# Two PSUM banks for the row products, one for the transposes, and an order that knows banks, in a fused attention and two-layer kernel

## The chip, the cores and the metric

The program runs on one core of a Trainium2 chip. The metric is the device time of one execution in microseconds (us): median of three runs for the kernel before, 859.1 us (858.09 to 859.74).

The engines are named as the profile names them: PE (matrix multiply), PEld (its weight loads), DVE (vector), ACT (scalar), POOL (GpSimd, which issues nearly all loads here) and SP (which issues DMA transposes and the last stores).

## What is computed

Block-causal attention over 4 batches of 8 heads (576 positions, head size 64), then two feed-forward layers over the 2304 tokens:

```python
scores = scale * np.matmul(q, k.transpose(0, 1, 3, 2))
scores = np.where(block_i >= block_j, scores, -1000000000.0)   # blocks of 64
attn = np.exp(scores - np.max(scores, axis=-1, keepdims=True))
attn = attn / (np.sum(attn, axis=-1, keepdims=True) + 1e-09)
x = np.matmul(attn, v)                     # 2304 tokens x 512
h = ((x @ w1) * (x @ w2)) @ w3             # 1024
x = h @ w_out                              # 512
r = np.maximum(x @ w_in, 0.0)              # 2048
out = (r * r) @ w2_out                     # 512
```

Weights come as float64 words and are turned into high and low parts on the chip, so a product is three matmuls (high x high, high x low, low x high).

## The kernel before

**Order.** Nothing is issued where the code stands. Every step is recorded in a list (`od.op`, class `Order`) with its engine, a cost, the keys it reads and writes, and a priority. At the end `Order.emit` plays the list through a small model of the engines: it takes the ready step with the lowest priority key on the engine that is free first, and issues it. So each engine has one fixed order of instructions, set by the costs in the model, and on the chip each engine runs its own list strictly in that order. A tile (`Buf`) belongs to a tag with a number of buffers; a new tile of a tag waits for the last user of the tile that many places before it. In the model of before two engines may work in one PSUM bank as long as the keys differ. On the chip they wait for each other there.

**Setup and batch 0.** The first attention pairs 0 to 3 (batch 0, two heads each) are `whole`: scores `s` on PE (line 825), maxima on DVE, exponentials on ACT (line 884), scaling by the reciprocal on DVE (line 910), transposes of the weights on PE (`tp`, line 968) into a PSUM bank, a copy of that bank to `pt` on ACT (line 974), then the product with v (`pv_bank`, line 1071). The transposes of one head and one group of query tiles come in two parts, each with its own `tp` tile. The tag `tp` has two banks, the tag `po` one.

Between them stand the rows `setup_rows(i)`, i = 0 to 7: row i of w3 times w_out, on PE at line 1108, output `po`, then copied out as a high part by ACT (line 1209) and a low part by DVE (line 1214) into `w3o`. Rows 0 to 2 use float32 operands, which show as two trace instructions for each matmul. Row 0 takes the whole `po` bank. Rows 1 to 5 take the same single `po` bank in two halves of 256 columns. Rows 6 and 7 and everything after take banks in turn from the two `tp` and the one `po` (`bank3`).

The 64-bit words of w_out (`wo`), w3 (`w3t`) and w1, w2 (`w`) are loaded by POOL, scaled on ACT (lines 325, 329, 478, 483) and joined on DVE. Where PE has nothing to do in the first 25 us the model issues `warm_up` matmuls (line 591), which compute nothing.

**Batches 0 to 3.** From about 122 us the products `ab` with w1 and w2 start, and attention of the next batch runs beside them. Each of the eight w1/w2 tiles needs a column sum on PE (line 357, input `wsum`) in the midst of the PE list.

**Second layer.** From about 490 us the 2304 rows of y are worked off in blocks c = 0 (256 columns) and c = 1 to 4 (512 columns), each in eight steps j. Blocks 2 to 4 use seven products instead of eight (`h_winograd`, line 1866; `out_strassen`, line 2034). `y_load(c)` makes from the loaded y the parts b11, b21, t1, t2, t3, t4, b22, each as a high part (ACT, line 275) and a low part (DVE, line 277); each part has one buffer, which every block uses again.

## Time and profile before

| what | value |
|---|---|
| median of three runs | 859.1 us |
| the profiled execution | 859.63 us |
| its span, first to last instruction | 857.9 us |
| PE busy | 834.0 us (97%) |
| DVE busy | 704.3 us (82%) |
| ACT busy | 605.3 us (71%) |
| POOL busy | 111.4 us (13%) |

PE is the engine that is nearly always busy. A row of the timeline reads: start, length, engine, line, operation, output and inputs with shapes, how many instructions are merged, and in brackets the idle time ahead of the first of them with what ended it. Matmul rows are modelled at their ends and overlap a little.

### The profile page before, as it was taken

To read this page: it belongs to the slowest core of one execution; us is meant where nothing else is said; L and a number is where in the kernel's file an instruction comes from. 1 tells how busy PE (TensorE), PEld (TensorE's weight loads), DVE (VectorE), ACT (ScalarE), POOL (GpSimd) and SP (SyncE) were. 2 spreads that over 40 slices of the span, in tenths; PEclk is the share of its full clock that TensorE was granted. 3 is DMA by queue.
4 is the path that set the end of the run, shared out by engine and by line. 5 is a ranking of instruction groups with operands and counts; after the bars stand their busy time and mean duration, and the time that the engine had idled before them with its cause. 6 is when DMAs were issued, how large, how long until landed. Compare 5 with 4: busy or idle time off the path is not lost. (4 is left out here: it accounts for less than half of the span.)

```text
span 857.9 us, 19317 instructions
## 1 busy us (share of the span) xinstructions
PE 834.0 (97%) x7504; PEld 676.9 (79%) x7504; DVE 704.3 (82%) x1643; ACT 605.3 (71%) x1393; POOL 111.4 (13%) x206
## 2 busy tenths in 40 slices
PE   8999999999999999999999999999999999999997
PEld 6567776778878888789979878666678888888886
DVE  5988989997787787864788899999979798797775
ACT  5988888976677676764999985756755654664562
POOL 5111211111211112001322101010020001001000
PEclk9999999999999999999999999999999999999999
DMA  8942465699998999772665512020030002001001
GB/s 312 339 150 93 135 176 161 143 182 191 215 178 159 196 154 202 134 148 77 210 193 191 176 50 74 26 100 2 1 109 16 1 2 74 2 1 51 1 2 50
DMA packets 104830, 100.23 MB, mean 117 GB/s; under 512 B 83041, under 2 KB 86881, under 8 KB 103329
## 3 DMA queue, kind: packets, MB, share of 16 engines
q0 software_dynamic: 18144, 71.18, 26.5%
q1 hardware_dynamic: 86592, 27.80, 19.1%
q8 instruction: 59, 0.97, 0.5%
q14 instruction: 35, 0.28, 0.1%
HBM read 62.78 MB, written 9.44 MB: 84 GB/s over the span
## 5 line engine op out<-in xcount | busy, mean ns | idle before, releaser
L1108 PEld LDWEIGHTS <-w 128*128 128x128 f16 x1536 | 146.8, 98 | 43.7 <-issue 5.9
L884 ACT ACTIVATE pf<-s,nm 128x192 f32<-128x192 f32 (+4 forms) x160 | 82.4, 524 | 44.0 <-DVE nm L867 39.5
L1108 PE MATMUL ab<-x0h,w 128*128 128x320 f16 x512 | 108.9, 299 | 0.5 <-DVE w L287 0.3
L1108 PE MATMUL y<-g,w3o 128*128 128x320 f32 (+1 forms) x768 | 108.3, 298 | 0.0
L1108 PEld LDWEIGHTS y<-g,w3o 128*128 128x128 f32 x768 | 103.1, 188 | 2.1 <-issue 1.2
L1108 PE MATMUL ab<-x1h,w 128*128 128x256 f16 x512 | 88.7, 273 | 0.0
L2034 PEld LDWEIGHTS <-gs 128*128 128x128 f16 x816 | 78.9, 98 | 11.4 <-DVE gs L277 2.2
L1866 PEld LDWEIGHTS <-wb 128*128 128x128 f16 x768 | 75.1, 98 | 15.2 <-issue 3.8
L1108 PE MATMUL ab<-x0l,w 128*128 128x320 f16 x256 | 76.5, 299 | 0.7 <-DVE x0l L1033 0.7
L1929 ACT ACTIVATE c<-c,beta 128x512 f32<-128x512 f32 x48 | 34.2, 713 | 58.4 <-DVE c L1898 58.4
L932 DVE SCALAR_TENSOR_TENSOR p<-pf,r,p 128x192 f16<-128x192 f32 (+2 forms) x120 | 63.0, 546 | 12.5 <-ACT p L925 11.2
L1108 PE MATMUL ab<-x1l,w 128*128 128x256 f16 x256 | 69.8, 272 | 0.0
L2161 PE MATMUL o<-wb,g 128*128 128x512 f16 x288 | 66.7, 379 | 0.6 <-DVE c L2171 0.6
L925 ACT ACTIVATE p<-pf,r 128x192 f16<-128x192 f32 (+2 forms) x120 | 62.0, 556 | 6.6 <-DMA pt<-p 3.7
L2034 PE MATMUL p<-ts,gs 128*128 128x256 f16 x480 | 61.8, 273 | 0.1
L1866 PEld LDWEIGHTS <-st 128*128 128x128 f16 x576 | 56.1, 98 | 6.7
L825 PE MATMUL s<-kraw,qraw 64*128 64x288 f32 (+4 forms) x384 | 56.5, 411 | 0.4 <-ACT pf L884 0.2
L2161 PEld LDWEIGHTS <-g 128*128 128x128 f16 x288 | 27.9, 98 | 30.3 <-issue 0.9
L825 PEld LDWEIGHTS s<-kraw,qraw 64*128 64x128 f32 x384 | 34.2, 186 | 17.1 <-issue 8.3
L2034 PE MATMUL p<-wb,gs 128*128 128x256 f16 x336 | 44.7, 273 | 0.2 <-DVE gs L277 0.2
L859 DVE TENSOR_REDUCE nm<-s 128x2 f32<-128x384 f32 (+1 forms) x64 | 42.3, 683 | 1.0
L338 DVE CUSTOM_DVE_ANT_0 cx<-raw,cx 128x1024 uint16<-128x1024 uint16 (+1 forms) x53 | 39.0, 737 | 4.5 <-ACT raw L329 2.3
(265 smaller groups left out, 1977.4 us busy)
## 6 DMA issues: line engine op xcount, KB each, us to landing
raw<-in_wb POOLq DMA_DIRECT2D x32, 512.0 KB, 5.5
raw<-in_w3t POOLq DMA_DIRECT2D x8, 1024.0 KB, 10.0
raw<-in_w POOLq DMA_DIRECT2D x16, 512.0 KB, 4.8
yraw<-ydram POOLq DMA_DIRECT2D x12, 512.0 KB, 4.5
vraw<-in_vp POOLq DMA_DIRECT2D x16, 320.0 KB, 5.3
qraw<-in_qT POOLq DMA_DIRECT2D x16, 288.0 KB, 4.7
kraw<-in_kT POOLq DMA_DIRECT2D x32, 144.0 KB, 5.9
vmix<-v SPq DMA_DIRECT2D x24, 160.0 KB, 5.0
```

The source lines that it names most:

```text
L338: dve.tensor_tensor(out=x(), in0=x(), in1=words()[1], op=ALU.add)
L825: pe.matmul(o[:, h] if t == 4 else o, q()[rows, q_start(t) : q_start(t) + 128], keys_()[rows, c], start=True, stop=True,)
L859: lambda k=k, t=t, nm=nm, banks=banks: dve.tensor_reduce(out=nm()[:, k], in_=banks[0]()[:, :, S_COL[t] : S_COL[t] + n_keys(t)], op=ALU.max ...
L884: act.activation(o, view(a, t), AF.Exp, bias=nm()[:, k, a : a + 1], scale=SCALE, accum_out=ssum()[:, k, a : a + 1],)
L925: lambda o=o, nk=nk, a=a, k=k, w=weights, p16=p16, r=r: act.activation(p16()[:, o : o + nk], w(a, k), AF.Copy, scale=r()[:, k, a : a + 1]),
L932: lambda o=o, nk=nk, a=a, k=k, w=weights, p16=p16, r=r: dve.scalar_tensor_tensor(out=p16()[:, o + nk : o + 2 * nk], in0=w(a, k), scalar=r( ...
L1108: pe.matmul(acc(), l, r, start=k == 0, stop=k == len(mms) - 1)
L1866: pe.matmul(acc()[:, TH * half : TH * half + TH], lhs(a, kc), y[yn]()[:, kc], start=n == 0, stop=n == len(mms) - 1,)
L1929: lambda src=src, k=k: act.activation(src(), src(), AF.Relu, scale=beta()[:, j, k : k + 1]),
L2034: pe.matmul(acc()[:, TH * u : TH * u + TH], t()[:, o : o + P], r(b), start=first and n == 0 and u == tiles[0], stop=last and n == 2 and u ...
L2161: pe.matmul(o(), g[gx]()[:, cols], wt(f)[:, a, 512:1024], start=(begin and n == 0), stop=(last and n == 2),)
```

## The change

1. `PSUM_POOLS`, `Op.banks`, `at` and `held`: the model keeps, for each PSUM bank, until when each engine works in it, and lets no other engine start there before.
2. `c_first`: a faster cost for loads (0.55 to issue, 0.00245 per KB, 2.3 to land, before 0.6, 0.0033 and 4.0), for the loads of batch 0's q, k and v and the wide weight loads.
3. k of a pair comes by one transfer of 128 partitions, not two of 64.
4. The tag `po` has two banks, `tp` has one. Rows 0 to 5 take a whole bank each and are no longer halved. `bank3` goes round `po`, `po`, `tp`.
5. For blocks 3 and 4 of the second layer `y_load` has the key `K_LOAD`, so its steps may stand from the middle of the block before. Block 3's b11, b21 and t3 have homes of their own (`OTHER_HOMES`).
6. In `h_winograd` the product with t3 stands after those with b21 and t2.

```diff
+        def at(o):
+            t = o.ready
+            for b in o.banks:
+                for e, until in held.get(b, {}).items():
+                    if e != o.eng and until > t:
+                        t = until
+            return t
...
-                start = max(t0, min(o.ready for o in todo))
-                o = min((o for o in todo if o.ready <= start), key=lambda o: (o.key, o.n))
+                start = max(t0, min(at(o) for o in todo))
+                o = min((o for o in todo if at(o) <= start), key=lambda o: (o.key, o.n))
...
+            for b in o.banks:
+                held.setdefault(b, {})[eng] = o.end + self.WAIT
...
+    def c_first(kb):
+        return (0.55, kb * 0.00245, 2.3)
...
-        for a in range(2):
-            rows = slice(64 * a, 64 * a + 64)
-            od.op(
-                GQ, c_dma(144), lambda rows=rows, n=2 * p + a: pool.dma_start(out=k()[rows], in_=kT[n][0:64]),
-                [], [(k, a)], key,
-            )
+        both = slice(2 * p * P + P // 2, 2 * p * P + P // 2 + P)
+        od.op(GQ, (c_dma if p >= KDM else c_first)(288), lambda: pool.dma_start(out=k(), in_=k_rows[both]), [], [(k, 0), (k, 1)], key)
...
-            tp = buf("pm", "tp", 2, [P, 512], F32, f"tp_{name}_{part}")
+            tp = buf("pm", "tp", 1, [P, 512], F32, f"tp_{name}_{part}")
...
-        tag, n = ("po", 1) if n_bank3[0] % 3 == 0 else ("tp", 2)
+        tag, n = ("tp", 1) if n_bank3[0] % 3 == 0 else ("po", 2)
...
-        if not i:
-            po_bank.append(buf("pm", "po", 1, [P, 512], F32, "po"))
-        for half in range(2) if 0 < i < PO_SPLIT else (None,):
+        if i < PO_SPLIT:
+            po_bank.append(buf("pm", "po", 2, [P, 512], F32, f"po_{i}"))
+        for half in (None,):
...
-                acc = Half(po_bank[0], cols, range(2) if half is None else (half,))
+                acc = Half(po_bank[i], cols, range(2) if half is None else (half,))
...
+        K_LOAD = [K_EVICT if c < 3 else K_B + 2 * (KP * (c - 1) + 5) + 0.55 for c in range(len(BLOCKS))]
...
+        OTHER_HOMES = {
+            "b11": ("wp", "ysq", 1, 1), "b21": ("wp", "ysc", 1, 1), "t3": ("mo1", "a", 2, 2),
+        }
...
-            split_half(h, l, src, 2 * TH, ([(h,)], [(l,)], [key]), K_EVICT)
+            split_half(h, l, src, 2 * TH, ([key_of(h)], [key_of(l)], [key]), K_LOAD[c])
...
             product(b17, 0, w_of(0, 0), "b11")
-            product(b17, 1, s_of(3), "t3")
...
             product(b26, 1, s_of(2), "t2")
+            product(b17, 1, s_of(3), "t3")
```

The new cost model moves instructions on every engine. Three places follow. In the names, the numbers at the end are the program's own.

ACT of before, after the exponentials of pair 0 (`pt` copies a transposed bank out, `raw` converts loaded words; raw_99 is w3's row 0, raw_163 and raw_170 the first block of w_out):

```order
L974 ACTIVATE pt_0_0_264<-tp_0_0_0_255 128x384
L974 ACTIVATE pt_0_0_264<-tp_0_0_1_260 64x256
L478 ACTIVATE raw_99<-raw_99 128x1024
L483 ACTIVATE raw_99<-raw_99 128x1024
L974 ACTIVATE pt_0_1_299<-tp_0_1_0_281 128x384
L974 ACTIVATE pt_0_1_299<-tp_0_1_1_292 64x256
L974 ACTIVATE pt_1_0_340<-tp_1_0_0_316 128x384
L884 ACTIVATE pf_2_0_344,ssum_2_345<-s_2_0_269,nm_2_289 128x576
L478 ACTIVATE raw_163<-raw_163 128x512
```

The same place on ACT of the changed kernel (raw_98 is w3's row 0, raw_150 and raw_155 the first block of w_out):

```order
L991 ACTIVATE pt_0_0_243<-tp_0_0_0_237 128x384
L498 ACTIVATE raw_98<-raw_98 128x1024
L503 ACTIVATE raw_98<-raw_98 128x1024
L498 ACTIVATE raw_150<-raw_150 128x512
L503 ACTIVATE raw_150<-raw_150 128x512
L498 ACTIVATE raw_155<-raw_155 128x512
L503 ACTIVATE raw_155<-raw_155 128x512
L991 ACTIVATE pt_0_0_243<-tp_0_0_1_296 64x256
L264 ACTIVATE wo_328<-wox_0_305 128x512
L991 ACTIVATE pt_0_1_335<-tp_0_1_0_320 128x384
```

The copy of the second part of the first head moved behind six conversions, four of them of words that come from w_out's first block.

PE of before, at row 1 of the row products (po), between attention pair 1's transposes (tp):

```order
L1108 MATMUL po<-wox_1_508,w3x_297 128x512
L968 MATMUL tp_0_0_0_535<-ident,pf_0_0_476 128x128 x3
L968 MATMUL tp_0_0_1_542<-ident,pf_0_0_476 64x128 x2
L968 MATMUL tp_0_1_0_552<-ident,pf_0_1_515 128x128 x3
L1108 MATMUL po<-wox_0_360,w3x_532 128x256
L1108 MATMUL po<-wox_1_382,w3x_532 128x256
L1108 MATMUL po<-wox_0_436,w3x_532 128x256
L1108 MATMUL po<-wox_1_440,w3x_532 128x256
L968 MATMUL tp_0_1_1_568<-ident,pf_0_1_515 64x128 x2
```

PE of the changed kernel, at the end of row 0 and the start of row 1:

```order
L985 MATMUL tp_2_0_1_458<-ident,pf_2_0_368 64x128
L1125 MATMUL po_353<-wox_0_423,w3x_287 128x512
L1125 MATMUL po_353<-wox_1_428,w3x_287 128x512
L985 MATMUL tp_2_1_0_474<-ident,pf_2_1_380 128x128 x4
L1125 MATMUL po_483<-wox_0_305,w3x_447 128x512
L1125 MATMUL po_483<-wox_1_332,w3x_447 128x512
L985 MATMUL tp_2_1_1_497<-ident,pf_2_1_380 64x128
L1125 MATMUL po_483<-wox_0_360,w3x_447 128x512
L1125 MATMUL po_483<-wox_1_362,w3x_447 128x512
```

Each part of a head's transposes now stands apart from the next, with a pair of row products between, and row 1 has another bank (po_483) than row 0 (po_353).

DVE of before, where block 2 of the second layer ends (names with _2_7) and block 3 starts (_3_0); b11l, b21l, t1l, t2l are low parts of block 3's y:

```order
L277 TENSOR_TENSOR b11l_10076<-yraw_73_9433,b11h_10013 128x512
L277 TENSOR_TENSOR b21l_10085<-yraw_74_9421,b21h_10035 128x512
L1898 TENSOR_TENSOR c_2_7_10024<-p_2_7_10069,c_2_7_10024 128x256
L277 TENSOR_TENSOR t1l_10096<-t_3_9566,t1h_10059 128x512
L277 TENSOR_TENSOR t2l_10106<-t_3_9595,t2h_10044 128x512
L277 TENSOR_TENSOR gs_9470<-c_2_7_10057,gs_9470 128x512
L1543 TENSOR_TENSOR yraw_74_9421<-yraw_74_9421,t_3_9595 128x2x256
L1940 TENSOR_TENSOR c_2_7_10024<-c_2_7_10024,c_2_7_10057 128x256
L1898 TENSOR_TENSOR c_3_0_10136<-p_3_0_10117,x_3_0_10125 128x256
L1940 TENSOR_TENSOR s_2_7_10146<-c_2_7_10024 128x512
L1898 TENSOR_TENSOR c_3_0_10136<-p_3_0_10117,x_3_0_10125 128x256
```

DVE of the changed kernel at the same place:

```order
L297 TENSOR_TENSOR t1l_9959<-t_3_9444,t1h_9939 128x512
L297 TENSOR_TENSOR t2l_9968<-t_3_9474,t2h_9910 128x512
L1936 TENSOR_TENSOR c_2_7_9912<-p_2_7_9952,c_2_7_9912 128x256
L297 TENSOR_TENSOR t4l_9979<-yraw_74_9297,t4h_9929 128x512
L297 TENSOR_TENSOR b22l_9989<-yraw_74_9297,b22h_9970 128x512
L297 TENSOR_TENSOR gs_9346<-c_2_7_9942,gs_9346 128x512
L1978 TENSOR_TENSOR c_2_7_9912<-c_2_7_9912,c_2_7_9942 128x256
L1978 TENSOR_TENSOR s_2_7_10019<-c_2_7_9912 128x512
L297 TENSOR_TENSOR gs_9346<-c_2_7_9912,gs_9346 128x512
L1936 TENSOR_TENSOR c_3_0_10036<-p_3_0_10002,x_3_0_10009 128x256 x2
```

The low parts of b11 and b21 and the subtraction into yraw have left the place (they stand four steps earlier, at _2_3), and t4l and b22l have come into it. On PE the product of step 1 of block 3, which stood before the end of step 7 of block 2, now stands behind it.

## Rows read from the trace of the kernel before

**Rows 1.** The page: busy time, share and instructions of each engine.
```profile
PE 834.0 (97%) x7504; PEld 676.9 (79%) x7504; DVE 704.3 (82%) x1643; ACT 605.3 (71%) x1393; POOL 111.4 (13%) x206
```

**Rows 2.** Busy time by stretch; last three columns: granted clock, DMA share, GB/s.
```profile
core 0: us, PE busy (x) PEld busy (x) DVE busy (x) ACT busy (x) POOL busy (x), PEclk, DMA share, GB/s
0.00:25.00 25.00, 20.57 (x208) 16.51 (x209) 15.38 (x44) 15.47 (x39) 12.75 (x29) 1.00 0.89 327
25.00:62.00 37.00, 33.69 (x178) 22.53 (x180) 31.78 (x65) 32.89 (x64) 5.71 (x9) 0.95 0.67 243
62.00:125.00 63.00, 61.15 (x494) 48.35 (x491) 54.30 (x139) 53.03 (x139) 11.46 (x22) 1.00 0.41 123
125.00:200.00 75.00, 70.12 (x676) 55.00 (x676) 69.33 (x186) 61.76 (x157) 11.03 (x21) 1.00 0.76 164
200.00:448.00 248.00, 247.11 (x2606) 205.29 (x2602) 183.47 (x462) 179.63 (x478) 42.49 (x80) 1.00 0.82 171
```

**Rows 3.** The warm-up matmuls (line 591) alone, columns PE and PEld, then as in Rows 2.
```profile
0.00:25.00 25.00, 8.57 (x107) 7.98 (x107) 1.00 0.89 327
```

**Rows 4.** Waits of PE over the whole span: total us, times, longest.
```profile
PE p L1866 <- DVE c L1898: 2.9, 3, 1.3
PE po L1108 <- DVE w3o L1214: 2.4, 5, 0.6
PE tp L968 <- ACT pt L974: 2.1, 3, 1.4
PE pv_bank L357 <- DVE wsum L406: 1.7, 2, 1.3
...
PE po L1108 <- ACT w3o L1209: 0.5, 1, 0.5
```

**Rows 5.** Timeline of PE, 24 to 48 us: transposes and row products.
```profile
27.89 1.98 PE L1108 MATMUL po<-wox,w3x 128*128 128x512 f32 x4
...
37.88 0.55 PE L968 MATMUL tp<-ident,pf 128*128 128x128 f32 x3 [1.42 <-ACT pt L974]
```

**Rows 6.** Stretches around the idle time at 37.9 us, columns as in Rows 2.
```profile
36.00:39.10 3.10, 1.44 (x9) 0.91 (x9) 3.10 (x6) 3.10 (x6) 0.00 (x0) 1.00 1.04 294
39.20:42.50 3.30, 3.30 (x10) 2.51 (x9) 2.46 (x4) 1.92 (x5) 0.53 (x1) 0.50 0.36 151
```

**Rows 7.** Timeline of POOL, first loads.
```profile
1.96 1.05 POOL L627 DMA_DIRECT2D kraw<-in_kT  x2
...
12.28 0.53 POOL L471 DMA_DIRECT2D raw<-in_wo  x1 [0.31 <-issue]
```

**Rows 8.** The page, DMA issues of w_out's first block: KB each, us to landing.
```profile
raw<-in_wo POOLq DMA_DIRECT2D x2, 512.0 KB, 5.5
```

**Rows 9.** Timeline of ACT, 12.9 to 21 us.
```profile
12.97 0.76 ACT L974 ACTIVATE pt<-tp 128x384 f32<-128x384 f32 x2
...
19.33 0.65 ACT L478 ACTIVATE raw<-raw 128x512 f32<-128x512 f32 x1
19.87 0.67 ACT L483 ACTIVATE raw<-raw 128x512 int32<-128x512 uint32 x1
```

**Rows 10.** Copies of transposed banks, 20 to 125 us: ns min/median/max.
```profile
L974 ACT ACTIVATE pt<-tp x43: 255/426/610, 20.4 to 109.8; 128x384 f32<-128x384 f32 x13, 64x192 f32<-64x192 f32 x8, 128x512 f32<-128x512 f32 x8, 64x128 f32<-64x128 f32 x8
```

**Rows 11.** Timelines of PE and DVE where block 2 ends and block 3 starts.
```profile
688.93 0.27 PE L1866 MATMUL p<-b11h,wb 128*128 128x256 f16 x1
...
690.90 0.27 PE L1866 MATMUL p<-t1h,wb 128*128 128x256 f16 x1
...
692.96 0.27 PE L1866 MATMUL p<-b11h,wb 128*128 128x256 f16 x1 [1.25 <-DVE c L1898]
...
687.29 0.68 DVE L277 TENSOR_TENSOR b11l<-yraw,b11h 128x512 f16<-128x512 f32 x1
...
692.50 0.41 DVE L1898 TENSOR_TENSOR c<-p,x 128x256 f32<-128x256 f32 x1
```

**Rows 12.** Timeline of PE where block 3 ends and block 4 starts.
```profile
768.09 0.27 PE L1866 MATMUL p<-b11h,wb 128*128 128x256 f16 x1 [1.29 <-DVE c L1898]
```

More of the change, by code (lines that the diff above doesn't have):

```diff
@@ L45, in n_keys @@
     return 128 * t + 64
+PSUM_POOLS = ("ps", "pm", "mb")
 class Buf:
@@ L70, in __init__ @@
         self.deps = set()
+        self.banks = ()
         self.left = 0
@@ L113, in op @@
         o.deps.discard(o)
+        o.banks = tuple(dict.fromkeys(k[0] for k in (*r, *w) if isinstance(k[0], Buf) and k[0].pool in PSUM_POOLS))
         self.ops.append(o)
@@ L129, in emit @@
         free, avail, dma = {}, {}, 0.0
+        held = {}
+        def at(o):
[5 more added lines that the diff above has]
+            return t
         for n, o in enumerate(self.ops):
@@ L316, in convert @@
         ku, kw = (raw, "u"), (raw, "l")
-        od.op(GQ, c_dma(n), lambda: pool.dma_start(out=raw(), in_=src), after, [ku, kw], key)
+        od.op(GQ, (c_first if wide is not None else c_dma)(n), lambda: pool.dma_start(out=raw(), in_=src), after, [ku, kw], key)
         def words():
@@ L470, in joined @@
         ku, kw = (raw, "u"), (raw, "l")
-        od.op(GQ, c_dma(n), lambda: pool.dma_start(out=raw(), in_=src), [], [ku, kw], key if load is None else load)
+        od.op(GQ, c_first(n), lambda: pool.dma_start(out=raw(), in_=src), [], [ku, kw], key if load is None else load)
         def word(k):
@@ L559, in spare @@
         return 0.0 if p < KDM else SPARE_1 if p < 2 * KDM else SPARE
+    k_rows = kT.rearrange("n p s -> (n p) s")
     raws = {}
@@ L581, in fused_kernel @@
     table = buf("at", "table", 1, [P, 1], F32, "table")
-    warm_out = buf("pm", "po", 1, [P, 512], F32, "warm_out")
+    warm_out = buf("pm", "po", 2, [P, 512], F32, "warm_out")
     warm_cost = [0.11]
@@ L621, in load_pair @@
         q = at_buf("q", 2, [P, S], F32, f"qraw_{p}")
-        od.op(GQ, c_dma(288), lambda: pool.dma_start(out=q(), in_=qT[p]), [], [(q,)], key)
+        od.op(GQ, (c_dma if p >= KDM else c_first)(288), lambda: pool.dma_start(out=q(), in_=qT[p]), [], [(q,)], key)
         k = at_buf("k", 2, [P, S], F32, f"kraw_{p}")
-        for a in range(2):
-            rows = slice(64 * a, 64 * a + 64)
-            od.op(
-                GQ, c_dma(144), lambda rows=rows, n=2 * p + a: pool.dma_start(out=k()[rows], in_=kT[n][0:64]),
-                [], [(k, a)], key,
-            )
+        both = slice(2 * p * P + P // 2, 2 * p * P + P // 2 + P)
+        od.op(GQ, (c_dma if p >= KDM else c_first)(288), lambda: pool.dma_start(out=k(), in_=k_rows[both]), [], [(k, 0), (k, 1)], key)
         v = at_buf(*(("v16", 2) if p in (2, 3) else ("vraw", V_BUFS)), [P, NTILE, 2, D], F32, f"vraw_{p}")
         key = VKEYS[p] if p < KDM else key
-        od.op(GQ, c_dma(320), lambda: pool.dma_start(out=v(), in_=vp[p]), [], [(v,)], key)
+        od.op(GQ, (c_dma if p >= KDM else c_first)(320), lambda: pool.dma_start(out=v(), in_=vp[p]), [], [(v,)], key)
         raws[p] = q, k, v
@@ L1406, in second_block, with __init__, __call__, key_of @@
         cp_ = {}
-        def y_part(c, name):
+        OTHER_HOMES = {
+            "b11": ("wp", "ysq", 1, 1), "b21": ("wp", "ysc", 1, 1), "t3": ("mo1", "a", 2, 2),
+        }
+        class Piece:
+            def __init__(self, b, n):
+                self.b, self.n, self.key = b, n, (b, n)
+            def __call__(self):
+                return self.b()[:, self.n]
+        def key_of(t):
+            return t.key if isinstance(t, Piece) else (t,)
+        def y_part(c, name):
+            if c == FIRST_S + 1 and name in OTHER_HOMES:
+                *home, pieces = OTHER_HOMES[name]
+                if pieces == 2:
+                    return [buf(*home, [P, 2, TH], F16, f"{name}{n}_{c}") for n in "hl"]
+                t = buf(*home, [P, 2, 2, TH], F16, f"{name}_{c}")
+                return [Piece(t, n) for n in range(2)]
             home = "wp" if name in ("b11", "b21") else "w2"
@@ L1542, in sub @@
                     DVE, c_dve(2 * TH),
-                    lambda: dve.tensor_tensor(out=o(), in0=x(), in1=y(), op=ALU.subtract), r, w, K_EVICT,
+                    lambda: dve.tensor_tensor(out=o(), in0=x(), in1=y(), op=ALU.subtract), r, w, K_LOAD[c],
                 )
@@ L1773, in go @@
                         )
-                ks = both(f, 0) + [(t,) for x in ("b11", "b21") for t in ys_[c, x]]
+                ks = both(f, 0) + [key_of(t) for x in ("b11", "b21") for t in ys_[c, x]]
                 od.op(PE, len(mms) * c_mm16(TH), go, ks, [(acc,)], key)
@@ L1869, in go @@
                         )
-                od.op(PE, len(mms) * c_mm16(TH), go, ks + [(t,) for t in y], [(acc, half)], key, spare * strassen)
+                od.op(PE, len(mms) * c_mm16(TH), go, ks + [key_of(t) for t in y], [(acc, half)], key, spare * strassen)
             if strassen:
```

## The prediction

> **What bounds the kernel now.** I read the busy times of the page first [rows 1]: PE is busy 834.0 of 857.9 us, DVE 82%, ACT 71%. PE's own work is almost the same before and after, so the time can fall only by what PE loses: its idle time, warm-up matmuls that compute nothing, and time at the lower of its two clock levels. The table by stretch tells where these are [rows 2]. Until 25 us PE idles 4.4 us, and the 107 warm-ups fill another 8.6 us with empty work [rows 3]; that is the time until weights have come and been converted. From 25 to 62 us PE idles 3.3 us, from 62 to 125 us 1.9 us, from 125 to 200 us 4.9 us. From 200 to 448 us it idles 0.9 us in 248. The waits name the rest [rows 4]: 2.4 + 0.5 = 2.9 us for the two engines that empty the bank of a row product, 2.1 us for copies of transposed banks, 1.7 us for column sums of w1 and w2 on DVE alone, and 2.9 us in the second layer on DVE, of which two gaps make 1.25 + 1.29 = 2.5 us [rows 11, 12].
>
> I sum against the profiled execution (859.63 us, 1.7 us of it outside the span) and subtract 0.5 at the end, by which it lies above the median of 859.1. A measurement here can tell about 0.2%, or 1.7 us, from no change.
>
> **Rows in two banks.** Before, half of a row waits until DVE has read the other half out of the same bank. After, row i+1 has the other bank, and row i's bank is wanted again only two rows later. All six waits of PE for w3o go: -2.9 us [rows 4]. The bounds are -2.9 and 0 (if the rows then wait for what comes after, below). The halves become whole: 64 instructions of 256 columns become 32 of 512 in rows 1 and 2. Four of 512 take 1.98 us with the switch to other work and back [rows 5]; the columns are the same in number, so I count nothing. ACT and DVE save a fixed part in five copies each, under 0.5 us, off the path.
>
> **One bank for transposes.** Before, a head's two parts went out back to back into two banks. After, the second part must wait until ACT has copied the first. A copy takes 0.43 us, at most 0.61 [rows 10]. The order puts at least a pair of row products or a score product between them nearly everywhere, and a pair of row products covers 1.7 us or more (four instructions in the trace, 1.98 us with switches, [rows 5]). So the copy is covered while ACT is on time. While ACT is late it is not, and then even two banks did not help: the longest such wait, 1.42 us at 37.9 us, came with two banks [rows 5]. I charge +1.0 us, two waits of about a copy each, between 0 and 24 heads x groups x 0.43 = +10.3 us; I stay near the lower end, because the cover is there in the order. The Trainium skill (Perfetto Trace Analysis, Matmuls) says that independent matmul groups should rotate through PSUM banks so that the copy out overlaps the next group. That speaks for the rows' two banks and against the transposes' one; by it alone the two would cancel, and it doesn't weigh what stands between. No run here shows the transposes with one bank.
>
> **The long wait and the clock.** The wait of 1.42 us stands where ACT is full (3.10 of 3.10 us, [rows 6]) and three transpose parts stand together before row 1. Soon after it the granted clock is 0.50, that is 1.2 GHz, for 3.3 us in which PE is always busy [rows 6], so half of that, some 1.7 us, is lost. In the new order these parts stand apart, with row products between them. I count both as gone: -1.4 - 1.7 = -3.1 us, with 0 as the other bound.
>
> **Start.** k by one transfer: its second half was issued 0.5 us after the first (two in 1.05 us, [rows 7]), and the first scores wait for it, so the chain begins up to 0.5 us earlier (bounds -0.5 and 0; I take -0.5). Against it: ACT's copy of the first head's second part stood at 13.3 us (the second of two in 0.76 us from 12.97, [rows 9]) and now stands behind the conversions of w_out's first block. The last of those words are issued at 12.3 us and take 5.5 us [rows 7, 8], so they are there at about 17.8 us; with 0.65 + 0.67 us for two conversions [rows 9] the copy starts at 19.1 us, 5.8 us later. With one bank the next transposes wait for it too. Little of this lands on the end, since PE has only warm-ups to do there and the row products come sooner in exchange (w_out's words are converted first). Bounds 0 and +5.8; I take +2.0, since the attention work that is put off must be made up while ACT has little slack (busy 32.9 of 37 us, [rows 2]). Together +1.5 us.
>
> **125 to 200 us.** If PE comes here earlier, DVE must come earlier too, but it is busy 69.3 of 75 us [rows 2]. The lead so far is 2.9 + 3.1 - 1.0 - 1.5 = 3.5 us. DVE's idle time is 5.7 us here, and before it 5.2 (25 to 62) and 8.7 us (62 to 125), so part of the lead can be held. I give back a third, +1.2 us; bounds: the whole lead (+3.5) and, as the column sums are placed anew, a gain of the 4.9 us idle there. From 200 us on PE is full, and what is won stays won.
>
> **Second layer.** At the switch from block 2 to 3 DVE does four low parts and a subtraction before it comes to the sums that free a bank: c at 692.50 us, 0.41 us long, ends at 692.91, and PE starts at 692.96 [rows 11]. PE's next product stood ahead of the rest of block 2's work. In the new order b11, b21 and the subtraction are done four steps earlier, and step 1 of block 3 stands behind all of block 2's sums, so PE has some 10 us of products before it wants that bank. What is late next: the products of block 2's last step, which need gs. By the order DVE has six steps of 512 columns and two of 256 between 687.3 us and the gs with block 2's first sums; at 0.68 and 0.41 us, an upper bound because such rows overlap, these take 4.9 us, and with gs itself it is 692.9. PE reaches the first product that needs it after six products of block 3, from 688.93 us at 0.66 each (three take until 690.90, [rows 11]), also at 692.9. So nothing is left over, or 0.2 us. Both switches: -2.5 + 0.2 = -2.3 us; bounds -2.5 and 0. The rest of the 2.9 us stays, since blocks 0 to 2 keep their old key. The end of the kernel is untouched.
>
> **Sum.** -2.9 + 1.0 - 3.1 + 1.5 + 1.2 - 2.3 = -4.6 us: 859.6 - 4.6 = 855.0, less 0.5 is 854.5 us, 0.5% faster.
>
> **Rivals.**
> - *DVE holds the front.* The lead dies between 125 and 200 us, for DVE is at 92% there; only the second layer's 2.3 us stays: 859.1 - 2.3 = 856.8 us. For it speaks rows 2; against it DVE's 14 us of idle time from 25 to 125 us, which earlier row products and scores would fill.
> - *One transpose bank stops PE* (slower). Place: batch 0, 13 to 110 us. 24 second parts wait a copy of 0.43 us each behind a late ACT: +10.3 instead of +1.0, nothing given back later (-1.2), so 854.5 + 9.3 - 1.2 = 862.6 us. It decides from about 0.35 us for each part: 8.3 us are won by banks, clock and blocks, 1.5 lost at the start. For it: ACT has 4.1 us free from 25 to 62 us [rows 2]. Against it: the pair of row products between. This is the Trainium skill's rule (Perfetto Trace Analysis, Matmuls) taken against the transposes.
> - *The new order also closes 125 to 200 us.* A model that knows banks places column sums where they are ready: 4.9 us and the give-back go, 854.5 - 6.1 = 848.4 us. Nothing in the trace shows that the bank waits are behind those idle times, which end on DVE and ACT.
> - *It doesn't do what it says.* Rows and transposes wait as long as before, on ACT and DVE instead of the bank; start +1.5, second layer -2.3: 859.1 - 0.8 = 858.3 us.
>
> **How the numbers follow.** Forecast 0.48 (851.5 to 857.0), DVE holds the front 0.20, all closed 0.12, no effect 0.10, transposes stop PE 0.10. Faster by over 1.7 us is below 857.4: 0.48 + two thirds of 0.20 + 0.12 = 0.73. Within: the other third and nearly all of no effect, 0.16. Slower: 0.11. The range from 849.5 to 859.0 leaves out the transposes' case and half of the all-closed case, and a few hundredths of no effect: 0.8 is inside.
>
> **What would show it.** Right: no wait of PE for w3o, no granted clock under 1.0 between 25 and 62 us, no gap over 0.3 us at the two block switches, PE idle 125 to 200 us near 6 us. Wrong: waits of PE for pt beyond 2 us in total (the transposes), idle time of PE at the column sums beyond 7 us (DVE), or a loss before 25 us (idle plus warm-ups) beyond 15 us (the start). What would overturn the sum most cheaply is ACT: its list is in order, and a late load in it now stops copies that PE waits for.

## The result, and the profile after

The changed kernel takes 849.61 us in the median (847.38 to 849.90, four executions) against 858.96 us of the kernel before beside it. The ratio is 0.9886, with a 95% interval from 0.9867 to 0.9905: 9.3 us or 1.1% faster. The forecast was 854.5 us, 4.6 us faster, so the direction held and the size was half of what came. The time lies at the very lower end of the range, next to the rival in which the new order also closes the idle time from 125 to 200 us (848.4 us). The sections below show that this rival is not the reason either.

The page of the changed kernel, its row of busy times, to be held against [rows 1]:

```profile
PE 829.2 (98%) x7385; PEld 664.9 (78%) x7385; DVE 701.3 (83%) x1638; ACT 605.2 (71%) x1388; POOL 102.0 (12%) x190
```

PE is busy 829.2 of 848.1 us. The span is 9.8 us shorter; 5.0 us of that is idle time of PE and 4.7 us busy time. PE has 119 instructions fewer: 15 warm-ups, and 104 because rows 1 to 5 are no longer in halves. The next fence is the table by stretch of the changed kernel, with the columns of [rows 2]:

```profile
core 0: us, PE busy (x) PEld busy (x) DVE busy (x) ACT busy (x) POOL busy (x), PEclk, DMA share, GB/s
0.00:25.00 25.00, 17.52 (x151) 13.64 (x152) 15.47 (x42) 14.58 (x33) 11.79 (x27) 0.87 0.88 343
25.00:62.00 37.00, 36.84 (x206) 19.70 (x204) 33.67 (x68) 35.64 (x69) 3.77 (x7) 0.99 0.62 232
62.00:125.00 63.00, 60.80 (x434) 44.49 (x433) 57.48 (x146) 53.76 (x140) 10.73 (x20) 1.00 0.43 140
125.00:200.00 75.00, 73.70 (x699) 59.10 (x698) 68.23 (x191) 61.91 (x165) 10.31 (x19) 1.00 0.87 176
200.00:448.00 248.00, 245.82 (x2604) 202.54 (x2603) 184.94 (x465) 183.99 (x484) 38.97 (x73) 1.00 0.78 169
...
690.00:715.00 25.00, 25.00 (x231) 22.41 (x229) 23.33 (x47) 11.55 (x22) 2.92 (x5) 1.00 0.19 65
715.00:765.00 50.00, 50.00 (x459) 44.70 (x457) 40.50 (x86) 34.11 (x62) 0.00 (x0) 1.00 0.00 1
765.00:790.00 25.00, 25.00 (x231) 22.41 (x229) 17.50 (x37) 9.72 (x18) 2.16 (x4) 1.00 0.12 43
```

Four things are to be seen. Until 25 us PE idles 7.5 us instead of 4.4. From 25 to 62 us it idles 0.2 us instead of 3.3, and from 125 to 200 us 1.3 instead of 4.9. From 200 to 448 us it idles 2.2 us instead of 0.9, more than before. Around the two block switches it idles nothing.

The waits of PE over the whole span, columns as in [rows 4]:

```profile
PE tp L985 <- ACT pt L991: 2.3, 2, 2.1
...
PE y L1125 <- ACT g L264: 1.5, 1, 1.5
...
PE pv_bank L377 <- ACT junk L433: 1.0, 1, 1.0
PE pv_bank L377 <- DVE wsum L426: 0.8, 1, 0.8
```

There is no wait for w3o and none of the products `p` for c, the two that led [rows 4]. Of the 2.3 us of waits for pt, 2.1 us is one wait near the start. The wait for g is new.

To see where the time comes from, it helps to split both kernels at one point of the program: the last long run of `o` products before the second block of the second layer. Each pair of rows is a kernel's timeline of PE: this run, and the last products of the kernel. First before, then the changed kernel:

```profile
628.90 4.70 PE L2161 MATMUL o<-wb,g 128*128 128x512 f16 x21
...
852.14 1.47 PE L2034 MATMUL p<-ts,ring_a 128*128 128x256 f16 x12
```

```profile
622.33 4.70 PE L2199 MATMUL o<-wb,g 128*128 128x512 f16 x21
...
842.43 1.47 PE L2072 MATMUL p<-ts,ring_a 128*128 128x256 f16 x12
```

Up to this point the changed kernel is 6.57 us earlier; from there to the end it needs 220.10 us instead of 223.24, another 3.14 us. So two thirds of the gain lies in the first 630 us, where the first five terms of the forecast's sum came to 2.3 us.

The same stretch can be split by what PE does, each instruction counted until PE's next one starts and waits counted apart, as idle time. Up to these `o` products the changed kernel has 2.4 us less idle time, 2.1 us less in the row products, 1.7 in the scores, 0.7 in the warm-ups, 0.6 in the transposes and 0.3 in `ab`, and 1.3 us more in `y`. So less than half of the 6.6 us is idle time.

### The profile page after: what moved, and what is told of

Its sections match the earlier page's. It is cut to its first block, busy times and chain, and to the rows that moved or that the text cites. A ratio compares the mean times of both kernels' runs of the same rounds, so it can differ in the third digit from the quotient of the medians.

```text
span 848.1 us, 19077 instructions
## 1 busy us (share of the span) xinstructions
PE 829.2 (98%) x7385; PEld 664.9 (78%) x7385; DVE 701.3 (83%) x1638; ACT 605.2 (71%) x1388; POOL 102.0 (12%) x190
## 4 chain that ended last, share of the span: by engine, by line
PE 42%; DVE 9%; ACT 4%; issue 2%; DVEq 0%
PE p L1904 11%; PE p L2072 9%; PE ab L1125 8%; PE o L2199 6%; PE y L1125 6%; DVE c L1936 2%; ACT c L1967 2%; PE h L1808 2%; ACT c L1970 1%; DVE gs L297 1%; DVE c L1978 1%; DVE s L1978 1%; DVE u L1936 1%; ACT gs L295 1%; DVE t L2027 0%
## 5 line engine op out<-in xcount | busy, mean ns | idle before, releaser
L1125 PE MATMUL y<-g,w3o 128*128 128x320 f32 (+1 forms) x768 | 110.0, 299 | 1.8 <-ACT g L264 1.5
L842 PEld LDWEIGHTS s<-kraw,qraw 64*128 64x128 f32 x384 | 33.6, 186 | 15.6 <-issue 8.8
L295 ACT ACTIVATE gs<-c 128x512 f16<-128x512 f32 (+1 forms) x56 | 29.9, 535 | 18.2 <-DVE c L1978 18.1
```

The costliest lines, as they stand in the source:

```text
L295: od.op(ACT, c_act(n), lambda: act.activation(hi(), src(), AF.Copy), ks, kh, key)
L842: pe.matmul(o[:, h] if t == 4 else o, q()[rows, q_start(t) : q_start(t) + 128], keys_()[rows, c], start=True, stop=True,)
L1125: pe.matmul(acc(), l, r, start=k == 0, stop=k == len(mms) - 1)
```

## The experiments

The table has all fifteen runs: the median, that of the kernel before on the same chip, and the ratio with its 95% interval. "First" is how many microseconds earlier than the kernel before the run's trace reaches the last of the `o` products named above, and "second" how much less it takes from there to its last product; these two are from one profiled execution each. The ratio is taken over all executions, not from the two medians, so the two can differ a little (e12).

| run | us | before | ratio | first | second |
|---|---|---|---|---|---|
| e1: before, early y parts and moved product | 856.22 | 858.90 | 0.9961 (0.9940 to 0.9983) | -4.5 | 3.1 |
| e2: before, banks | 858.85 | 858.90 | 0.9992 (0.9973 to 1.0011) | 2.3 | -0.2 |
| e12: before, banks and order that knows them | 859.89 | 858.53 | 0.9998 (0.9973 to 1.0023) | -0.1 | -1.0 |
| e8: before, load times | 864.68 | 859.28 | 1.0073 (1.0042 to 1.0104) | -8.0 | 0.0 |
| e13: before, k by one | 857.56 | 859.51 | 0.9969 (0.9944 to 0.9994) | 1.1 | -0.1 |
| e14: before, banks and k | 852.16 | 859.51 | 0.9920 (0.9894 to 0.9946) | 6.9 | -0.1 |
| e15: before, banks, k, early y parts | 848.79 | 859.15 | 0.9885 (0.9865 to 0.9905) | 7.3 | 3.2 |
| e3: changed, old load times | 848.48 | 858.90 | 0.9857 (0.9816 to 0.9899) | 5.9 | 3.1 |
| e4: changed, order without banks | 850.70 | 858.90 | 0.9885 (0.9848 to 0.9922) | 5.5 | 3.1 |
| e5: changed, k by two | 851.95 | 859.28 | 0.9918 (0.9900 to 0.9935) | 4.3 | 3.1 |
| e6: changed, old split of banks | 862.68 | 859.28 | 1.0035 (1.0020 to 1.0049) | -5.3 | 3.1 |
| e7: changed, big loads later | 849.53 | 859.28 | 0.9887 (0.9870 to 0.9905) | 8.7 | 3.1 |
| e9: changed, rows in halves | 849.43 | 858.53 | 0.9870 (0.9824 to 0.9916) | 5.5 | 3.1 |
| e10: changed again | 849.23 | 858.53 | 0.9866 (0.9830 to 0.9902) | 6.8 | 3.1 |
| e11: changed, w_out and w3 later | 849.85 | 858.53 | 0.9875 (0.9839 to 0.9911) | 7.4 | 3.1 |

One profiled execution can differ from the median by a few microseconds, that of e1 above all (861.03 against 856.22 us: it lost some 6 us between 225 and 300 us, to waits of up to 2.8 us that the trace of before does not have; ahead of the longest, ACT waits 3.79 us for a DMA transpose to land) and that of e8 (868.73 against 864.68 us), so the verdicts go by the medians, and "first" is used where several traces agree.

**The second layer alone (e1).** The kernel before with these two parts of the change:

```diff
-            split_half(h, l, src, 2 * TH, ([(h,)], [(l,)], [key]), K_EVICT)
+            split_half(h, l, src, 2 * TH, ([key_of(h)], [key_of(l)], [key]), K_LOAD[c])
...
+            if c == FIRST_S + 1 and name in OTHER_HOMES:
+                *home, pieces = OTHER_HOMES[name]
...
-            product(b17, 1, s_of(3), "t3")
...
             product(b26, 1, s_of(2), "t2")
+            product(b17, 1, s_of(3), "t3")
```

> The kernel before with one part of the change alone: the early y parts of block 3 and the product that is moved behind block 2's last sums. The place theory (each part pays where its wait stood): the two gaps of 1.25 and 1.29 us at the block switches fall to under 0.3 us, nothing else moves, so about 2.5 us less than the kernel before: 856.5 us. The rival (the time there was only lent, since DVE is 92 % busy from 690 to 715 us): the gaps come back as waits for gs or for sums within the next 20 us, 858.5 to 859 us.

Measured: 856.22 us, 2.7 us less. The place theory holds, and firmly: in all ten traces of the table that have these parts, and in that of the changed kernel above, the stretch behind the `o` products is 3.1 or 3.2 us shorter, and in those without them it is not shorter, whatever the rest of the kernel is. Little of the gain comes back as another wait: behind this point PE waits 0.65 us in all for x in e1, and 0.5 us in the changed kernel.

**The banks alone (e2), and with an order that knows them (e12).** The edit of e2:

```diff
-        tp = buf("pm", "tp", 2, [P, 512], F32, f"tp_{name}_{part}")
+        tp = buf("pm", "tp", 1, [P, 512], F32, f"tp_{name}_{part}")
...
-        tag, n = ("po", 1) if n_bank3[0] % 3 == 0 else ("tp", 2)
+        tag, n = ("tp", 1) if n_bank3[0] % 3 == 0 else ("po", 2)
...
-        for half in range(2) if 0 < i < PO_SPLIT else (None,):
+        for half in (None,):
...
-                acc = Half(po_bank[0], cols, range(2) if half is None else (half,))
+                acc = Half(po_bank[i], cols, range(2) if half is None else (half,))
```

> The kernel before with the banks alone: two for the rows, rows whole, one for transposes; the order is still computed without knowledge of banks and with the old load times, k goes by two transfers. If the banks themselves bring the gain before 200 us: no wait of PE for w3o, the lead at 125 us over the kernel before is 4 to 6 us, and the time 853 to 855 us. If the gain needs the order to know what the banks cost: the waits for w3o (2.9 us) go, but waits for pt take at least as much, since the list that is emitted may set a head's two transposes back to back; lead at 125 us under 1 us, 858 to 861 us.

> The kernel before with the new split of banks and an order that knows banks; load times, k by two transfers and the second layer as before. The split alone measured 858.85 us against 858.9. If the knowledge of banks is what makes the split pay under the old load times: 854 to 856 us. If it is worth about 1 us here too, as under the new load times: 857 to 859 us, and what the run with the old load times had beyond the second layer comes from k by one transfer.

Measured: 858.85 and 859.89 us, no gain in either. Yet the traces show a lead where the banks work. I added up PE's work in the order of its instructions, each group of instructions at its mean time per column over the two traces, and read off when each kernel had done the same amount. Positive numbers say how many microseconds earlier than the kernel before a run is, at that kernel's time in the first column:

| us | changed | e2 | e14 | e3 | e7 | e6 | e8 |
|---|---|---|---|---|---|---|---|
| 25 | -3.5 | -0.4 | 0.1 | 0.1 | 0.9 | -0.2 | -4.3 |
| 62 | 2.5 | 3.2 | 3.8 | 3.7 | 6.7 | 2.1 | -6.2 |
| 110 | 6.6 | 6.4 | 6.7 | 6.5 | 10.5 | 3.9 | -7.8 |
| 140 | 4.8 | 3.3 | 4.4 | 4.3 | 7.4 | -3.8 | -7.3 |
| 225 | 8.6 | 5.7 | 6.0 | 5.5 | 8.5 | -4.1 | -7.4 |
| 350 | 8.3 | 4.7 | 6.5 | 6.0 | 8.5 | -4.9 | -8.7 |
| 400 | 6.0 | 2.5 | 6.5 | 6.0 | 8.8 | -5.0 | -8.7 |
| 640 | 6.6 | 2.3 | 6.9 | 5.9 | 8.7 | -5.3 | -8.0 |

At 110 us the banks alone (e2) lead by 6.4 us, as much as the changed kernel. So the first answer of its expectation is right up to there: the gain is there without knowledge of banks. It is given back later, from 110 to 140 us and between 350 and 400 us. Most of what goes between 350 and 400 us (2.2 us) goes in a wait for g; timeline of PE in e2, then its table by stretch:

```profile
377.34 0.41 PE L1130 MATMUL y<-g,w3o 128*128 128x320 f32 x1 [1.54 <-ACT g L264]
```

```profile
225.00:330.00 105.00, 103.90 (x1140) 84.92 (x1139) 81.38 (x214) 74.53 (x213) 15.29 (x29) 1.00 0.86 170
330.00:365.00 35.00, 35.00 (x398) 25.83 (x398) 27.51 (x69) 25.61 (x72) 3.73 (x7) 1.00 0.77 159
365.00:380.00 15.00, 13.24 (x141) 10.91 (x140) 9.52 (x24) 9.96 (x24) 1.11 (x2) 1.00 0.78 139
```

From 365 to 380 us PE, DVE and ACT are all free for a part of the time: the next product in PE's list waits for the chain from `ab` over two copies to g. The wait is one of order, not of a full engine.

**The load times (e3, e8).** e3 puts the old times into the changed kernel, e8 the new times into the kernel before:

```diff
     def c_first(kb):
-        return (0.55, kb * 0.00245, 2.3)
+        return c_dma(kb)
```

> The changed kernel, but its order computed with the old load times for batch 0 too. Theory that the load times close 62 to 200 us: the start is as good as before or better (idle and warm-ups before 25 us 13 to 14 us instead of 15.6), but PE idles again from 62 to 200 us, 5 to 7 us instead of 3.5, and the time is 852 to 855 us. Theory that banks and the order that knows them do: the time is 847 to 850 us, below the changed kernel by what the start gets back.

> The kernel before with its order computed with the measured load times of batch 0, nothing else. Theory that these close 125 to 200 us whatever the banks: PE idles there 1 to 2.5 us instead of 4.9, the start loses 2 to 3 us, and the time is 856 to 858 us. Rival, that this works only together with the second row bank: 125 to 200 us stays near 5 us idle, and the time is 859 to 862 us.

Measured: 848.48 us with the old times in the changed kernel, so the new ones bring it nothing; and 864.68 us with the new times in the kernel before, 0.7% slower and beyond both of its expectations. The first theory of e3 fell. In e8 PE waits more for what the banks decide, 4.2 us for pt against 2.1 before and 4.6 us for w3o (3.7 on DVE, 0.9 on ACT) against 2.9 [rows 4]; its waits of PE:

```profile
PE tp L990 <- ACT pt L996: 4.2, 3, 2.2
PE po L1130 <- DVE w3o L1236: 3.7, 7, 0.9
PE p L1909 <- DVE c L1941: 2.9, 3, 1.3
...
PE po L1130 <- ACT w3o L1231: 0.9, 2, 0.5
```

A part of e8's time is the clock: its two executions with a mean granted clock of 1.000 and 0.999 took 862.8 and 863.1 us, those with 0.993 and 0.994 took 868.7 and 868.8 us.

**The knowledge of banks (e4).** The order's record of banks is empty:

```diff
-        o.banks = tuple(dict.fromkeys(k[0] for k in (*r, *w) if isinstance(k[0], Buf) and k[0].pool in PSUM_POOLS))
+        o.banks = tuple(dict.fromkeys(k[0] for k in (*r, *w) if isinstance(k[0], Buf) and k[0].pool in ()))
```

> The changed kernel, but its order computed without knowledge of banks. Theory that the knowledge of banks does the work: waits of PE for pt of 3 us or more behind ACT's copies, and 853 to 856 us. Theory that the second row bank alone does it: no more than 1 us of new waits, 849 to 851 us.

Measured: 850.70 us; beside e10's 849.23 this is some 1.5 us, with intervals that overlap. PE's order is the same, instruction by instruction, until a column sum at 165 us; there PE waits 1.28 us instead of 0.35. In e3 and e14, of which e3 alone knows the banks, PE's order is the same up to the second layer's part, at 538 us; only ACT's and DVE's differ, from 167 us on. Together with e12 and e15 this says that the knowledge is worth 1 us or nothing, and that the lead at 110 us owes nothing to it.

**k by two again (e5), the old split again (e6), big loads later (e7).**

```diff
-        od.op(GQ, (c_dma if p >= KDM else c_first)(288), lambda: pool.dma_start(out=k(), in_=k_rows[both]), [], [(k, 0), (k, 1)], key)
+        for a in range(2):
+            rows = slice(64 * a, 64 * a + 64)
+            od.op(
+                GQ, (c_dma if p >= KDM else c_first)(144), lambda rows=rows, n=2 * p + a: pool.dma_start(out=k()[rows], in_=kT[n][0:64]),
+                [], [(k, a)], key,
+            )
```

> The changed kernel with k in two transfers of 144 KB again, the order computed anew for that. By subtraction of the first four runs (the banks alone gave nothing, the second layer 2.7 us, the load times nothing, the knowledge of banks about 1) the one transfer would carry some 4 us: 853 to 854 us. The rival, that it is worth only the half microsecond at the start and that the parts do not add up: 849 to 851 us.

> The changed kernel with the old split of banks: one for the rows, in halves of 256 columns, and two for the transposes; all else as changed. If whole rows in two banks are the main term (2.9 us of waits, and 2.4 us because a row in two halves takes 1.64 to 1.7 us on PE where a whole one takes 1.5): 855 to 857 us, with waits for w3o back and the row products again about 2.4 us longer in sum. If the order makes up for one bank, as it knows what it costs: 850 to 852 us.

> The changed kernel, but its order is computed with the loads of 512 KB and more landing 2.7 us later than it assumed, which is nearer to what the trace shows (w_out's first block landed at 15.7 us, the order assumed 12.8). This puts ACT's copy of the first head's second part back ahead of w_out's conversions. Theory that what the start loses stays lost: idle and warm-ups before 25 us fall from 15.6 to 13 or 14 us, and the time to 846 to 848 us. Rival, that the front makes it up by 110 us anyhow (the changed order with old load times was 3.5 us ahead of it at 25 us and level at 110 us): 849 to 850 us.

e5: 851.95 us, so k by one is worth 2.3 to 2.7 us in the changed kernel, between the two expectations. e6 undoes the diff of e2 in the changed kernel: 862.68 us, 13 us more than the changed kernel and slower than before. The term was expected at 6 us. Where it goes is seen in its trace, PE at 132.8 us and two stretches:

```profile
132.80 0.16 PE L377 MATMUL pv_bank<-wsum,ones 128*128 128x2 bf16 x1 [4.59 <-DVE wsum L426]
```

```profile
133.10:139.90 6.80, 5.60 (x21) 2.94 (x22) 4.48 (x14) 5.96 (x13) 0.54 (x1) 0.50 0.45 135
160.50:163.80 3.30, 2.85 (x11) 1.65 (x12) 3.09 (x10) 2.87 (x6) 0.00 (x0) 0.50 0.43 146
```

PE stands idle 4.59 us for one column sum, and then runs at half clock (0.50, that is 1.2 GHz) for 6.8 and once more for 3.3 us. With half of the busy time of the two spells (2.8 and 1.4 us) this is 8.8 us, against the 8.0 us that e6 loses between 110 and 225 us. Of w3o itself PE waits only 0.7 us in e6: that the old split sets this column sum where it stops PE is what the run shows, why it does so is not shown.

e7 changes one number, 2.3 to 5.0 for loads of 400 KB and more. The start is repaired: PE is at 25 us 4.4 us ahead of the changed kernel, with ACT's copy at 15.08 instead of 19.06 us. The first fence is e7, the second the changed kernel, both timelines of ACT:

```profile
15.08 0.38 ACT L991 ACTIVATE pt<-tp 64x256 f32<-64x256 f32 x1 [0.33 <-PE tp L985]
```

```profile
18.50 0.66 ACT L503 ACTIVATE raw<-raw 128x512 int32<-128x512 uint32 x1
19.06 0.36 ACT L991 ACTIVATE pt<-tp 64x256 f32<-64x256 f32 x1
```

The time is 849.53 us all the same. By 225 us the two are level (8.5 and 8.6 us in the table), so the rival of its expectation holds: what the start loses does not reach the end.

**Halves (e9), the changed kernel again (e10), a smaller repair of the start (e11).** e9 puts back the line `for half in range(2) if 0 < i < PO_SPLIT else (None,)`, with two banks; e11 uses the old load times in the loads of w_out and w3 alone.

> The changed kernel with two banks for the rows, but rows 1 to 5 in halves of 256 columns again, and its order computed anew for that. If the halves themselves cost PE time (the first runs show the row products 2.4 us shorter in sum where rows are whole): the row products take 2 to 2.5 us longer in sum, and the time is 851 to 853 us. If that is hidden or only the second bank counts: 849 to 850 us.

> The changed kernel unaltered, beside the other three on the same chip, so that differences under 2 us can be told: 849 to 850 us; the half clock shortly before 25 us in most executions, and a time about 2 us lower in those without it.

> The changed kernel, its order computed with the old load times for the first loads of w_out and w3 alone (these are the ones that ACT and DVE convert) and the measured ones for q, k and v. The copies that PE waits for stand ahead of the conversions again. If what the start loses counts at the end: 846 to 848 us, and no half clock before 25 us. If the front evens it out by 225 us, as in the run with the big loads late: 849 to 850 us.

e9: 849.43 us, the same as e10's 849.23. My expectation came from e1 against e2, where the row products took 53.8 against 51.4 us (each instruction counted until PE's next one starts, waits left out); in e9 they take 52.1 us, and whole rows in two banks 51.0 to 52.0 us in the runs whose clock is full there. So halves cost about 1 us at most. PE does not wait for w3o in e9, so the second bank takes these waits away with halves too. e11: 849.85 us, no gain from the start here either.

**k alone (e13), banks and k (e14), three parts (e15).** No new edits; these build up from the kernel before.

> The kernel before with k by one transfer alone, its order computed anew. If the transfer itself is worth something wherever it is put (without it the changed kernel took 2.3 us more): 855 to 857 us, and the first scores start by up to 0.5 us earlier. If it only changes the order by chance: 858 to 861 us.

> The kernel before with the new split of banks and k by one transfer; load times, knowledge of banks and second layer as before. The split alone led the kernel before by 6.4 us at 110 us and had 2.1 us left at the end of its profiled execution, none by the median. If the one transfer is what lets the lead be kept (the changed kernel with old load times kept 5.9 us of it until the second layer): 852 to 854 us. If the lead is given back here too: 857 to 859 us, and keeping it needs all parts of the order together.

> The kernel before with the new split of banks, k by one transfer and the second layer's part, and without the measured load times and the knowledge of banks. If these three are the whole of the change's gain: 849 us (852.16 for banks and k, less 2.7 to 3.1 for the second layer). If the order's knowledge adds to them: 850.5 us or more, and the change with its measured load times must be faster by that.

k alone: 857.56 us, 0.3% less, between its two expectations. Banks and k: 852.16 us, 7.4 us less, though the banks alone gave nothing and k alone 2. With the second layer's part as well: 848.79 us, all of the change's gain. The lead of e14 (table above) is that of e2 until 225 us. Then it stays, where e2 loses 3.4 us. The same stretches as above, e14:

```profile
225.00:330.00 105.00, 105.00 (x1174) 86.20 (x1174) 85.10 (x223) 74.96 (x213) 14.23 (x27) 1.00 0.93 174
330.00:365.00 35.00, 35.00 (x379) 25.56 (x374) 27.88 (x70) 27.33 (x79) 1.87 (x3) 1.00 0.76 156
365.00:380.00 15.00, 15.00 (x155) 13.29 (x153) 7.50 (x18) 8.23 (x18) 1.67 (x3) 1.00 0.78 156
```

PE does not idle at all from 225 to 380 us; e2 idles 2.9 us there. Why the order around 375 us has the hole in some lists is open. It is not k as such, for the changed kernel has k by one and has the hole too:

```profile
373.78 0.41 PE L1125 MATMUL y<-g,w3o 128*128 128x320 f32 x1 [1.53 <-ACT g L264]
```

The lists of e3, e5, e7, e9, e11, e14 and e15 do not have it. What one transfer saves is idle time of PE. Up to the `o` products e13 has 1.5 us less of it than the kernel before, e14 5.6 us less than e2, and the changed kernel 4.6 us less than e5, from one execution each. The loads that POOL issues behind k also land earlier: from w_out's first block on, those of w_out and w3 in the first 40 us land 0.3 to 1.3, 1.0 to 2.0 and 0.2 to 1.3 us earlier in these three pairs. No run separates the earlier loads from the new order that comes with them.

A version that beats the changed kernel by more than the measurement tells did not come of this: e15, e3 and e11 lie between 848.5 and 849.9 us.

## Why the prediction was half right, step by step

**Rows in two banks (-2.9): right on the waits, wrong to count the row products at nothing, and kept only with other parts.** All waits for w3o are gone. But the row products themselves, waits left out, fell from 55.3 to 53.2 us, each with a spell of the lower clock in it. Where the clock is full throughout them they take 52.6 to 54.6 us in one bank (e1, e6, e13) and 51.0 to 52.0 us whole in two (e2, e3, e5, e7, e11, e12, e14, e15). So a term of about 2 us stood at nothing, on the ground that the columns are the same in number; by e9 the wider products are 1 us of it at most. And e2 shows that the lead is no gain at the end by itself, e6 that going back to one bank costs 13 us once the order is computed with the new load times. A term for the banks alone does not exist.

**One bank for transposes (+1.0): the cover was right, the price too high.** The waits for pt are 2.3 us in the changed kernel and 2.4 us in e14, against 2.1 us before [rows 4]. That is over the 2 us named as the sign of a mistake, but 2.1 of the 2.3 us is the one wait for the late copy at the start. The rival in which this bank stops PE fell; the threshold worked out for it, about 0.35 us a part, leaves out the 1.5 us of the start (8.3 less 1.5 over 24 parts is 0.28), and nothing hangs on it. The Trainium skill (Perfetto Trace Analysis, Matmuls) says to rotate independent groups through PSUM banks. The traces agree for the row products (no wait for w3o with two banks, 2.9 us with one) and not for the transposes (0.2 us more with one bank than with two), between which the order puts other work.

**The long wait and the clock (-3.1): the wait went; the clock was read from one execution.** The wait of 1.42 us [rows 5] has no counterpart in the changed kernel. But e1 has the same PE order there, and the same wait, and its trace shows no lower clock behind it:

```profile
37.48 0.55 PE L990 MATMUL tp<-ident,pf 128*128 128x128 f32 x3 [1.40 <-ACT pt L996]
```

```profile
39.20:42.50 3.30, 3.30 (x18) 2.84 (x17) 3.08 (x5) 3.30 (x8) 0.53 (x1) 1.00 0.48 165
```

The granted clock is 1.00 where [rows 6] had 0.50. So the 1.7 us were not a property of the order, and the changed kernel has a spell of its own, at the start, of which half of the busy time is 3.0 us:

```profile
16.00:18.60 2.60, 0.69 (x10) 0.51 (x9) 2.25 (x8) 1.55 (x4) 0.84 (x2) 1.00 1.02 427
18.60:25.40 6.80, 5.93 (x22) 3.66 (x23) 4.61 (x9) 4.98 (x9) 1.24 (x3) 0.50 1.00 423
```

**Start (+1.5): the place was right, the carrying was wrong.** ACT's copy stands at 19.06 us, forecast 19.1, and PE waits 2.08 us for it. Idle time and warm-ups before 25 us are 15.6 us, over the 15 us that were named as the sign of a mistake. At 25 us the kernel is 3.5 us late, more than the 2.0 us forecast for it. But e7 and e11 repair the start and gain nothing. The step that failed is that the attention work put off must be made up later at PE's cost. The table tells where it was made up: e7 leads the changed kernel by 4.4 us at 25 us, still by 3.9 at 110, by 2.6 at 140, and by nothing at 225 us. So it went into time that e7 loses behind 110 us, 2.0 us of it idle time of PE: from 125 to 200 us PE idles 3.3 us in e7 and 1.3 us in the changed kernel.

**k by one transfer (-0.5): undersized.** Alone it measures 2.0 us, taken away from the changed kernel 2.3 to 2.7, and added to the banks 6.7 (858.85 to 852.16). The prediction counted the half microsecond between two issues in batch 0 and nothing for the other fifteen pairs of heads. The Trainium skill (DMA: Bandwidth & Descriptors, Rules for kernel authors) says that two transfers to disjoint halves of the partitions serialize and that one should be used. The sign agrees, and in the changed kernel the first scores start at 5.36 instead of 5.71 us. But what one transfer does to the later loads and the later order is larger than this. The trace of before has one wait of PE that ends with a k transfer, 1.35 us at 198.5 us, and a step of DVE that reads `pv_bank` ends there too.

**125 to 200 us (+1.2 given back): the step fell, its opposite is no cause.** In the changed kernel PE idles 1.3 us there instead of 4.9. But e3, e14 and e2 do give back 0.7 to 1.0 us between 110 and 225 us, as forecast, and e3 and e14 with e1's part (e15) end at the same time, though PE idles 3.3 us from 125 to 200 us in e15: the changed kernel loses 2.3 us again from 350 to 400 us. "What is won from 200 us on stays won" failed in e2 and in the changed kernel and held in e3, e7 and e14.

**Second layer (-2.3): right, a little small.** 2.7 us alone, 3.1 us by the traces. The 0.2 us that were put down for gs did not come, and a third gap of 0.3 us near 653 us that was to stay also went.

Put together: the sum had 2.3 us up to the second layer and 2.3 us in it. The second measured 3.1, the first 6.6 us by the trace, and there the prediction failed. Its premise that PE's own work is almost the same before and after, so that only idle time, warm-ups and the clock can fall, was wrong: idle time gave 2.4 of the 6.6 us, and the row products, counted at nothing, 2.1. By 110 us 6.6 us were won, not 3.5, with the start's loss still in them. The two costs in the sum, 1.5 us for the start and 1.2 us given back, were not paid in the end, for the lead is 6.6 us again at 640 us, while k's half microsecond was 2.3 to 2.7 us. That the time still lies inside the range, by 0.1 us, is luck.

What stays open is why the banks and the one transfer bring so much more together than apart, and why the scores take 1.7 us less in the changed kernel; in e14, which gains as much up to the second layer, they do not. The parts of the order do not add: 0 (banks) and 2 (k) make 7.4 together, and the load times cost 5.4 us before and nothing now.

## What to carry to other kernels

Where one cost model sets the order of thousands of instructions, a change of a bank, a transfer or a load time is a new order from there on: price its own place from the trace, but find its worth at the end by taking it away from the finished version as well as by adding it alone. A lead that is won early counts only if later stretches have no hole in the order, and a loss at the start only if no idle time lies behind it, however far behind. Changes in a place with little freedom, such as the block switches here, kept their price in every version.

## What was not expected of the hardware

The lower clock comes and goes between executions. In e1 and before, the same PE order up to 545 us and nearly the same wait (1.40 and 1.42 us) had the clock at 1.00 in one and 0.50 for 3.4 us in the other. Both profiled executions of the changed kernel have 0.50 for 6.8 us from 18.6 and 18.3 us on, and among its first four executions the one with a mean granted clock of 1.000 took 847.4 us, those with 0.996 849.6 to 849.9 us: some 2.3 us, a quarter of the change's gain. Among e10's six, those with 0.996 took 849.6 to 850.0 us, those with 0.997 and 0.999 took 848.2 to 848.8 us, some 1.4 us less. Before these spells PE had idled 1.9 of 2.6 us (changed kernel) and 4.59 us at a stretch (e6).

The loads land later than the size alone says: the order took w_out's first block to land at 12.8 us, and its first load landed at 15.6 us in the changed kernel. The next one, of 512 KB, and three of 1024 KB behind it landed 2.3 to 2.5 us apart, the small one no sooner than the large ones.
